# Loads, turns and stores as steps of a searched instruction order, in an attention and gated feed-forward kernel

## The chip, the cores and the metric

The kernel runs on one core of one Trainium2 chip. The metric is the device time of one execution in microseconds (us); the profile is one such execution, taken by the hardware profiler. Engines are called TensorE (PE), VectorE (DVE), ScalarE (ACT), GpSimd (POOL) and SyncE (SP). Each takes its instructions in the order in which the program lists them for it and waits on semaphores of the others.

## The reference

Input x has 4 batches of 12416 rows of 128; there are 32 inducing rows of 128. Two attention blocks and a gated feed-forward layer follow each other:

```python
def mab(q, kv):
    s = scale * (q @ kv.transpose(0, 2, 1))
    s = s - s.max(-1, keepdims=True)
    a = np.exp(s)
    a /= a.sum(-1, keepdims=True) + 1e-09
    return a @ kv
h = mab(I, x)          # per batch: 32 rows gathered from all of x
x1 = mab(x, h)         # every row of x attends to its batch's 32 rows
gate = np.maximum(x1 @ w_gate, 0.0)
val = x1 @ w_val
out = gate * val @ w_out      # 128 -> 1536 -> 128
```

So a batch's h needs all of that batch's x before any row of the batch's output can be made. The output has 49664 rows of 128 in float32.

## The kernel before

A row of x1 is a mix of only 32 rows of h, so gate times val is a quadratic form in 32 weights. The kernel uses this: for each batch it makes a table T (128 rows at a time, 8 groups of them) from h, the weights and their products, and an output tile is five matmuls of the exponentials of pairs of scores with T. This holds as long as the sign of each gate is the same for all rows of a batch; the kernel keeps a bound on that ("kept", "near"), and a general kernel stands behind a branch (L1071) that is not taken here.

**Tiles.** A batch is 97 tiles of 128 rows. Sixteen tiles make a quad q (0 to 5), the 97th tile is a small quad NQ = 6. Tiles are also counted in blocks of four (TPB), 25 blocks or slots to a batch (NSLOT).

**Stages of a batch.**
- *Load* (`load_x`, L86): a quad of x comes from HBM by a DMA that GpSimd issues, 512 KB in float32, cast on the way to the fp16 buffers x16 (nine, and two small ones).
- *Turn* (`turn_x`, L91): a quad is transposed from x16 to xT (twelve buffers) by a DMA transpose that SyncE issues. Three quads of batch 1 are turned on TensorE instead (`turn_pe`, L696).
- *First attention*: `score` (L704, L706) makes the exponentials of a quad against the inducing rows, `sums` (L716, L725) adds them up with x16, `h_end1`, `h_end2` make h.
- *Tables*: `gates`, `products` (L470), `joined` (L479), `fifth`, `table` (L516), `table5` (L536) make the next T.
- *Second attention*: `pair_scores` (L369), `pair_copy` (L634), `pair_reach` (L649), `pair_exp` (L664).
- *Outputs*: `scores` (L567, L574), called an E step, forms sums of pairs of scores for two blocks on TensorE and takes the exponential F on ScalarE. `outputs` (L589, L591), an O step, is one output tile: five matmuls into a third of an o_ps bank. After three tiles `outputs_end` divides by the sums on VectorE (L606, L607) into osb; a buffer osb holds six tiles and there are four of them. A full osb is stored by a DMA that GpSimd issues (L617), 384 KB; the last stores of all go by SyncE and ScalarE.

While the outputs of batch b are made, batch b + 1 is in its first attention and tables, and batch b + 2 is being loaded.

**The order.** The order of steps is a string, ORDER, found by a search outside the kernel. Each letter is one step: E and O as above; p takes the next step of the lane of first attention (turns on TensorE, scores, sums, h, gates, masks), u of the lane of products and tables, s of the pair scores and bounds, x of the pair exponentials. A loop at L869 walks the string and emits the instructions.

Loads, turns and stores are not in the string. They are put by hand into a dictionary `dmas`, keyed by slot, and are emitted when the first O step of that slot is reached (L875 to L877):

```python
g0 = (b - 2) * NSLOT + (0 if b > 2 else 6)
dmas[g0].append(begin)
for q in range(NCH):
    dmas[g0 + q].append(lambda q=q: load_x(b, q))
    dmas[g0 + 7 + q].append(lambda q=q: turn_x(b, turns[q]))
```

So batch 2 loads one quad per slot from slot 6 (tiles 24 to 48 of the whole run), with the small quad last, and turns one per slot after that (tiles 52 to 76), with the small quad first. Batch 3 loads at tiles 97 to 121 and turns at 125 to 149. A store is appended to the slot after the one in which its last tile falls. `begin` copies one element of the last turned quad of the batch before to a cell "landed" on GpSimd (L688), which makes GpSimd wait until that turn has landed before it issues the batch's first load.

The semaphores that an instruction waits for are put in by the framework from the buffers that it reads and writes.

Of the kernel before, what the change touches and what calls it, by code (L numbers as in the profile page):

```python
# [26 lines left out]
def quadratic_body(ctx, tc, x, inducing, moe_w_gate, moe_w_val, moe_w_out, out):  # L27
# [51 lines left out]
    def crange(q):  # L79
        return q * CT, min((q + 1) * CT, NT)  # L80
# [470 lines left out]
    NF = 20  # L551
    sel4 = sel.rearrange("p k m -> p (k m)").rearrange("p (j c) -> p j c", j=4)
    F, p2s, scs, osbs = {}, {}, {}, {}
    dmas = defaultdict(list)

    def scores(b, q, d, j):

# [38 lines left out]

    def outputs_end(b, t):
        i = t % 3
        g = b * NSLOT + t // TPB
        k = i + 1  # L600
        a = t - i
        if a % 6 == 0:
            osbs[0] = mt([P, 6, P], FP32, "osb", 4)
        osb, a6 = osbs[0], a % 6
        rz = mt([P, 3, 1], FP32, "rzo", 4)
        dve.reciprocal(out=rz[:, 0:k, :], in_=outputs.ps[:, 0:k, P : P + 1])  # L606
        dve.tensor_tensor(  # L607
            out=osb[:, a6 : a6 + k, :],
            in0=outputs.ps[:, 0:k, 0:P],
            in1=rz[:, 0:k, :].broadcast_to([P, k, P]),  # L610
            op=ALU.mult,
        )
        if a6 == 3 or t == NT - 1:
            t0 = a - a6
            last = b == B - 1 and t >= NT - 8
            queue = pool if not last else act if t == NT - 1 else nc.sync
            store = lambda: queue.dma_start(  # L617
                out=ov[b][:, t0 : t + 1, :], in_=osb[:, 0 : t + 1 - t0, :]
            )
            if last:  # L620
                store()
            else:
                dmas[g + 1].append(store)

    def pair_scores(b, q):

# [39 lines left out]
        )  # L666


    lanes = {"p": [], "u": [], "s": [], "x": []}

    def plan_scores(b):
        for q in range(0 if b else 1, NCH):
# [8 lines left out]
    def plan_phase1(b):  # L681

        s = state[b]

        def begin():

            s["x16"], s["xT"] = {}, {}
            pool.tensor_copy(out=landed, in_=state[b - 1]["xT"][2 if b == 2 else NQ - 1][0:1, 0, 0:1])  # L688

        def turn_pe(q, k):  # L690

            if k == 0:
                s["xT"][q] = new_xT(q)
            ps = bank("m", "xT_ps", [P, 8, P], FP16)
            for t in range(8):
                nc.tensor.transpose(ps[:, t, :], s["x16"][q][:, 8 * k + t, :], eye16)  # L696
            dve.tensor_copy(out=s["xT"][q][:, 8 * k : 8 * k + 8, :], in_=ps)

        def score(q):
            t0, t1 = crange(q)  # L700
            n = t1 - t0
            ps = bank("m", "s1_ps", [P, CT, M])
            for t in range(n):
                nc.tensor.matmul(ps[:, t, :], s["xT"][q][:, t, :], indT, start=True, stop=True)  # L704
            p1 = s["p1", q] = mt([P, CT, M], FP16, "p1", 3)
            act.activation(out=p1[:, 0:n, :], in_=ps[:, 0:n, :], func=AF.Exp, scale=sm_scale)  # L706

        def sums(q, first):

            t0, t1 = crange(q)  # L710
            n = t1 - t0
            k = M * min(n, 4)
            ps = bank("m", "hz_ps", [P, C + 1])
            p1 = s["p1", q]
            for t in range(0, n, 4):
                nc.tensor.matmul(  # L716
                    ps[0:k, C : C + 1],
                    p1[:, t : t + k // M, :].rearrange("p t m -> p (t m)"),
                    ones16[:, 0:1],
                    start=t == 0,  # L720
                    stop=t + 4 >= n,
                )
            for t in range(n):
                r = t % 4
                nc.tensor.matmul(  # L725
                    ps[32 * r : 32 * r + 32, 0:C],
                    p1[:, t, :],
                    s["x16"][q][:, t, :],
                    start=t < 4,
                    stop=t + 4 >= n,  # L730
                )
            if first:
                s["hz"] = mt([P, C + 1], FP32, "hz", 1)
                dve.tensor_copy(out=s["hz"], in_=ps)
            else:
                dve.tensor_tensor(out=s["hz"][0:k, :], in0=s["hz"][0:k, :], in1=ps[0:k, :], op=ALU.add)

        def h_end1():
            zs = mt([P, M], FP32, "zs", 1)
            dve.tensor_scalar(  # L740
                out=zs,
                in0=stackI,
                scalar1=s["hz"][:, C : C + 1],
                scalar2=1.0,
                op0=ALU.mult,
                op1=ALU.mult,
            )
            s["h_ps"] = bank("m", "h_ps", [P, 2, M])
            nc.tensor.matmul(s["h_ps"][:, 0, :], s["hz"][:, 0:C], stackI, start=True, stop=True)
            nc.tensor.matmul(s["h_ps"][:, 1, :], ones32, zs, start=True, stop=True)  # L750

        def h_end2():
            halves(b, s["h_ps"][:, 0, :], s["h_ps"][:, 1, :])

        turns = [NQ] + list(range(NQ))
        if b == 1:
            dmas[0] += [lambda q=q: turn_x(b, q) for q in turns[0:4]]
            lanes["p"] += [lambda h=h: turn_pe(3 + h // 2, h % 2) for h in range(6)]
            order = (3, 4, 5, NQ, 0, 1, 2)
            at = (3.5, 5.5, 7.5, 7.8, 8.5, 10.5, 12.5)  # L760
        else:
            g0 = (b - 2) * NSLOT + (0 if b > 2 else 6)
            dmas[g0].append(begin)
            for q in range(NCH):
                dmas[g0 + q].append(lambda q=q: load_x(b, q))
                dmas[g0 + 7 + q].append(lambda q=q: turn_x(b, turns[q]))
            order = (0, NQ, 1, 2, 3, 4, 5)
            at = [(2.3 if b == 2 else 3.5) * k for k in range(NCH)]
        todo = []
        for q, h in zip(order, at):  # L770
            todo.append((h, lambda q=q: score(q)))
            todo.append((h + 2, lambda q=q, h=h: sums(q, h == at[0])))
        lanes["p"] += [g for h, g in sorted(todo, key=lambda u: u[0])]
        lanes["p"] += [h_end1, h_end2]

        def gates(w, a, odd, k):
            ps = bank("m", "hw_ps", [P, BLK])
            gates_pe(b, w, k, ps)
            units = slice(k * (NFF // 2), (k + 1) * (NFF // 2))
            gates_out(act, ps.unsqueeze(1), a[:, units, :], 0)  # L780
            gates_out(dve, ps.unsqueeze(1), odd[:, units, :], 1)

        f = lambda g, *args: lambda: g(*args)
        lanes["p"] += [f(gates, *w, k) for w in ((wg, ga, gb), (wv, va, vb)) for k in range(2)]
        lanes["p"] += [lambda: (gate_sum(b, 0), signs(b)), f(gate_sum, b, 1), f(masked, b)]

        todo, late = [], []
        for j in range(4):
            for odd in range(2):
                for i in range(2):  # L790
                    todo.append(f(products, i, 0, NFF, 4 * j, 4 * j + 4, odd))
            todo.append(f(joined, j))
            late.append((len(todo) + 1, f(table, b, j)))
            if j == 1:
                todo += [f(fifth, b, 0), f(fifth, b, 1)]
                late.append((len(todo) + 1, f(table5, b)))
        for n, g in late[::-1]:
            todo.insert(n, g)
        lanes["u"] += todo
# [69 lines left out]
    for step in ORDER:  # L869
        if step == "E":  # L870
            scores(*next(units))
        elif step == "O":
            b, t = next(tiles)
            g = b * NSLOT + t // TPB
            if t % TPB == 0:  # L875
                for f in dmas.pop(g, []):
                    f()  # L877
            outputs(b, t)
            if g == B * NSLOT - 3 and t % TPB == 0:
                cond = nc.values_load(flag.left[0:1, 0:1])  # L880
        else:
            lanes[step].pop(0)()
    assert not any(lanes.values()) and not dmas and next(tiles, None) is None
    return cond


ORDER = (
    "pEpEOsEpEOOEpOEOpxOEEOuppOOEEOpsOpOEEpsOOpOEEOppOOOOEEppOOOpxsEEOOOOpEEspOOpEOOEOOEpEOpO"
    "EEpxOOOOpEEssOOOOpOEpOOEpOOOOppEEsOOEOOpEOxOOusOOEEOuOOOuEuOEOOxOOOEuEOuOOOOEsEuOuuOxEEO"
    "OuuOEsEOOEpuOuEEupupOOuEEupOuuOpOxOOEEpuOupOOOEEOpuupOEuuEuOpOuEEssOOxpOOEEspOOOEpOOEEpO"  # L890
    "OpExpEOOOOEppOOOOEEsOOOOpOEEOpOOOpOEEOpOOOpEOOEOuOOOxEuEOOOuOOuEOxOusEEOOOOusuEEOOOuOEsO"
    "OOuuuEExOOOOOuOEEuOsOuOOEEOuOuEOOxupuEEuspOOOupEEppOuOEEOuOxOuOEEpsOpOOOEEpOOOpEEOuuOOps"
    "EOEOupOsEEOuOxOOpEEpxOOOOOOEEpOOOOEOEppEOOEOOpsEExOOOOOOEEsOpOOOEEOOppOOOEEOpOOOOEpOEOxp"
    "OOOuOEEOOuOOuEOuOExOuOOOEuEOOOuEuEsOOsuOEOEOuuOEOsEuOuOsEEOOuOOOEsEuOOOEuxEEuuOOOEEuOOOO"
    "sEEOOuOOEOEuOuuOEEOOOOuEOOuEuOOxOOEEOuOsEEOxOOOOOEEOOOOOOEExOOOOOOEEsOOOEOEOOOOOEEOOOOEO"
    "OEsOEOEOOOOEEOOOxOOOEEOOOOOOEEOOOxOOOEEOOOssEOOEOOOEsEOOOOEOOEOOxOOEEsOOOOOEEsOOOOsOxEEO"
    "OOOOOOOOOOO"
)


# [202 lines left out]
```

## Time and profile before

| | |
|---|---|
| time, median of three | 279.61 us (279.19 to 279.83) |
| span of the profiled execution | 278.5 us |
| TensorE busy | 251.6 us |
| ScalarE busy | 228.1 us |
| VectorE busy | 214.5 us |
| GpSimd busy | 62.1 us |
| DMA moved | 48.38 MB, of it 38.08 MB on GpSimd's queue and 9.16 MB on SyncE's |
| E steps on ScalarE (L574) | 192 of 1025 ns |
| output tile on VectorE (L606, L607) | 132 of 175 ns and 132 of 550 ns, three tiles each |

The page gives busy time by engine, then the span in 40 slices of 7 us with the busy share of each in tenths, the clock that TensorE was granted, and the busy share of the 16 DMA engines. The list of waits says for each engine's instruction what released it: "DVE osb L607 <- DMA out_dram<-osb: 2.4, 1, 2.4" is 2.4 us in all, once, the longest 2.4. "issue" is time in which an engine waited for nothing that the profile shows. The first output tile starts at 39.3 us, the last at about 271 us.

### The profile page before, as it was taken

The page shows a single profiled execution, that of the slowest core. Times are in us where ns is not written, and L with a number is a line of the kernel's source. Part 1 is how long each engine was busy: PE and PEld are TensorE (multiplying, and loading weights), DVE is VectorE, ACT ScalarE, POOL GpSimd, SP SyncE. Part 2 cuts the span into 40 slices and gives each one's busy share as a digit, 9 for nine tenths or more (in the row PEclk, how much of TensorE's full clock was granted, in tenths as well). Part 3 has the DMA queues.
Part 4 walks back from the last instruction along what each step waited for, and adds up shares of the span by engine and source line. Part 5 has one row for each costly group of instructions (what it writes and reads, how often), then busy time and mean ns, then how long its engine had stood idle before and what let it go on. Part 6 is the DMA issues. An engine that isn't in the chain of part 4 may idle for free.

```text
span 278.5 us, 9515 instructions
## 1 busy us (share of the span) xinstructions
PE 251.6 (90%) x4029; PEld 187.7 (67%) x4029; DVE 214.5 (77%) x583; ACT 228.1 (82%) x305; POOL 62.1 (22%) x134
## 2 busy tenths in 40 slices
PE   2995799999899979998699999999999999999970
PEld 0793667777666657766387776777676777687760
DVE  4666977687899958888569989599989997767660
ACT  4235899999899969998478999999999999999930
POOL 8471000223231100431113011112121222121300
PEclk9999999999999999999779999999999999999997
DMA  7999979999979999899799992322422343424242
GB/s 184 200 208 204 214 144 143 205 201 213 244 250 203 159 209 231 162 230 261 231 218 230 149 212 112 125 114 115 172 94 79 121 174 118 169 115 172 115 170 79
DMA packets 44434, 48.38 MB, mean 174 GB/s; under 512 B 35472, under 2 KB 36272, under 8 KB 44384
## 3 DMA queue, kind: packets, MB, share of 16 engines
q0 software_dynamic: 11936, 38.08, 51.5%
q1 hardware_dynamic: 32160, 9.16, 22.4%
q8 instruction: 33, 0.54, 0.8%
q10 hardware_dynamic: 288, 0.46, 0.5%
q14 instruction: 17, 0.14, 0.1%
HBM read 27.80 MB, written 25.43 MB: 191 GB/s over the span
## 4 chain that ended last, share of the span: by engine, by line
PE 67%; DMA 8%; DVE 8%; ACT 7%; issue 5%; POOL 2%; POOLq 0%; DVEq 0%; ACTq 0%
PE o_ps L589 27%; PE e_ps L567 13%; PE o_ps L591 6%; ACT F L574 5%; DMA out_dram<-osb 4%; DMA xT<-x 4%; DVE osb L607 3%; PE s_ps L704 2%; PE T_ps L516 2%; PE xT_ps L259 2%; PE T_ps L502 2%; PE s_ps L369 2%; PE hz_ps L725 2%; PE s_ps L270 1%; PE xT_ps L696 1%
## 5 line engine op out<-in xcount | busy, mean ns | idle before, releaser
L574 ACT ACTIVATE F<-e_ps 128x1024 f16<-128x1024 f32 x192 | 185.6, 1025 | 19.9 <-PE e_ps L567 16.6
L589 PE MATMUL o_ps<-T,F 128*128 128x129 f16 x1536 | 130.5, 223 | 7.4 <-DVE osb L607 5.3
L589 PEld LDWEIGHTS <-F 128*128 128x128 f16 x1536 | 99.9, 98 | 33.9 <-issue 20.6
L591 PE MATMUL o_ps<-T,p 128*128 128x129 f16 x388 | 85.3, 220 | 0.0
L607 DVE TENSOR_TENSOR osb<-o_ps,rzo 128x384 f32<-128x384 f32 x132 | 72.5, 550 | 6.9 <-DMA out_dram<-osb 2.4
L617 POOL DMA_DIRECT2D out_dram<-osb x65 | 35.7, 549 | 187.9 <-DVE osb L607 110.4
L567 PE MATMUL e_ps<-sc,sel 32*128 32x512 f16 x384 | 59.1, 386 | 0.6
L606 DVE RECIPROCAL rzo<-o_ps 128x3 f32<-128x3 f32 x132 | 23.1, 175 | 22.7 <-PE o_ps L591 21.1
L591 PEld LDWEIGHTS <-p 128*128 128x128 f16 x388 | 38.4, 99 | 0.4
L567 PEld LDWEIGHTS <-sel 32*128 32x128 f16 x384 | 15.7, 91 | 18.0 <-issue 5.2
L634 DVE TENSOR_SCALAR sc<-s_ps 128x512 f16<-128x512 f32 (+1 forms) x28 | 17.6, 628 | 1.9 <-PE s_ps L369 1.9
L649 DVE TENSOR_REDUCE reach<-sc 128x1 f32<-128x512 f16 (+1 forms) x28 | 17.6, 627 | 1.3 <-POOL reach L648 0.3
L664 ACT ACTIVATE p<-sc 128x512 f16<-128x512 f16 (+1 forms) x28 | 16.4, 585 | 0.0
L272 ACT ACTIVATE p<-s_ps 128x256 f16<-128x256 f32 (+3 forms) x16 | 5.3, 333 | 10.9 <-PE s_ps L270 10.9
L260 DVE COPY xT<-xT_ps 128x1024 f16<-128x1024 f16 (+2 forms) x15 | 8.8, 584 | 4.5 <-PE xT_ps L259 3.2
L706 ACT ACTIVATE p<-s_ps 128x512 f16<-128x512 f32 (+1 forms) x21 | 11.3, 546 | 0.4 <-PE s_ps L704 0.2
L479 DVE TENSOR_TENSOR U<-U,U 128x1536 f16<-128x1536 f16 (+1 forms) x12 | 10.8, 903 | 0.2
L516 PE MATMUL T_ps<-wo,U 128*128 128x128 f16 x144 | 10.5, 224 | 0.2 <-DVE sc L634 0.2
L704 PE MATMUL s_ps<-indT,xT 128*128 128x32 f16 x288 | 10.0, 177 | 0.2 <-DMA xT<-x 0.2
L86 POOL DMA_DIRECT2D x<-in_x_dram x18 | 9.7, 544 | 1.8 <-DMA wg<-in_moe_w_gate_dram 1.3
L704 PEld LDWEIGHTS <-xT 128*128 128x128 f16 x288 | 8.9, 96 | 1.6 <-issue 0.9
L369 PE MATMUL s_ps<-xT,h 128*32 128x512 f16 x96 | 9.4, 387 | 0.4 <-DVE gb L361 0.4
(159 smaller groups left out, 248.2 us busy)
## 6 DMA issues: line engine op xcount, KB each, us to landing
out_dram<-osb POOLq DMA_DIRECT2D x62, 384.0 KB, 3.9
x<-in_x_dram POOLq DMA_DIRECT2D x18, 512.0 KB, 10.3
x<-in_x_dram POOLq DMA_DIRECT2D x8, 256.0 KB, 7.6
out_dram<-osb SPq DMA_DIRECT2D x2, 384.0 KB, 2.9
x<-in_x_dram POOLq DMA_DIRECT2D x5, 128.0 KB, 8.3
osb<-in_x_dram ACTq DMA_DIRECT2D x1, 384.0 KB, 4.5
osb<-in_x_dram SPq DMA_DIRECT2D x1, 384.0 KB, 4.3
wg<-in_moe_w_gate_dram POOLq DMA_DIRECT2D x1, 384.0 KB, 8.3
```

The costliest lines, as they stand in the source:

```text
L516: nc.tensor.matmul(ps, u_cols(0, t, j), wo[:, t, :], start=t == 0, stop=t == NFF - 1)
L567: nc.tensor.matmul(ps[:, r, :], sel4[rows, j, :], sc[rows, :], start=True, stop=True)
L574: act.activation(out=F[b, q, d, j], in_=ps, func=AF.Exp, scale=sm_scale2)
L589: nc.tensor.matmul(ps, f, T[b % 2][:, j, 0 : P + 1], start=j == 0, stop=False)
L591: nc.tensor.matmul(ps, p2s[b, q][rows, tok], T[b % 2][rows, 4 + r, 0 : P + 1], start=False, stop=True)
L606: dve.reciprocal(out=rz[:, 0:k, :], in_=outputs.ps[:, 0:k, P : P + 1])
L607: dve.tensor_tensor(out=osb[:, a6 : a6 + k, :], in0=outputs.ps[:, 0:k, 0:P], in1=rz[:, 0:k, :].broadcast_to([P, k, P]), op=ALU.mult,)
L617: store = lambda: queue.dma_start(out=ov[b][:, t0 : t + 1, :], in_=osb[:, 0 : t + 1 - t0, :])
L634: dve.tensor_scalar(out=scs[b, q][0:k, 0:w], in0=ps[0:k, 0:w], scalar1=64.0, scalar2=-64.0, op0=ALU.min, op1=ALU.max,)
L649: dve.tensor_reduce(out=state[b]["reach"][0:k, q : q + 1], in_=scs[b, q][0:k, 0:w], axis=AX.X, op=ALU.max, apply_absolute_value=True,)
L664: act.activation(out=p2s[b, q][0:k, 0:w], in_=scs[b, q][0:k, 0:w], func=AF.Exp, scale=sm_scale2)
L704: nc.tensor.matmul(ps[:, t, :], s["xT"][q][:, t, :], indT, start=True, stop=True)
```

## The change

Loads (letter l) and turns (t) become steps of the string; stores are emitted where their last tile ends; and the string is the result of a new search in which, by the change's own words, stores and output buffers are modelled and turned quads are allowed to land late. `dmas` and `begin` are gone.

- A load step takes the next quad in the order NQ, 0, 1, ... 5. If a turn was issued since the last load, GpSimd first waits for the latest one by the copy to "landed".
- A turn step turns the quad that was loaded last of those not yet turned (`s["loaded"].pop()`).
- Scores and sums take the quads in the order in which they were turned, not in a fixed one. The first quad summed is one that was turned first; if that were the small one, hz would be cleared.
- Batch 1's four turns by DMA are emitted before the loop.

| | before | after |
|---|---|---|
| steps | 388 O, 191 E, 82 u, 75 p, 40 s, 27 x | the same, 14 l, 14 t |
| E steps alone, in pairs | 73, 59 | 83, 54 |
| batch 2 loads before tile | 24, 28, 32, 36, 40, 44, 48 | 18, 18, 18, 18, 22, 67, 70 |
| batch 2 turns before tile | 52, 56, 60, 64, 68, 72, 76 | 44, 50, 51, 55, 57, 89, 91 |
| batch 2 scores before tile | 81, 82, 86, 90, 94, 99, 104 | 71, 76, 86, 91, 97, 114, 123 |
| batch 3 loads before tile | 97, 101, 105, 109, 113, 117, 121 | 104, 105, 111, 113, 120, 163, 166 |
| batch 3 turns before tile | 125, 129, 133, 137, 141, 145, 149 | 133, 141, 151, 151, 155, 184, 191 |
| batch 3 scores before tile | 168, 171, 171, 178, 184, 189, 194 | 166, 172, 188, 194, 207, 210, 216 |
| first, last table step of batch 1's u lane, tile | 74, 97 | 62, 93 |
| of batch 2's | 147, 191 | 161, 194 |
| of batch 3's | 248, 290 | 248, 290 |

```diff
-    dmas = defaultdict(list)
...
-            store = lambda: queue.dma_start(
-                out=ov[b][:, t0 : t + 1, :], in_=osb[:, 0 : t + 1 - t0, :]
-            )
-            if last:
-                store()
-            else:
-                dmas[g + 1].append(store)
+            queue.dma_start(out=ov[b][:, t0 : t + 1, :], in_=osb[:, 0 : t + 1 - t0, :])
...
-        def begin():
-            s["x16"], s["xT"] = {}, {}
-            pool.tensor_copy(out=landed, in_=state[b - 1]["xT"][2 if b == 2 else NQ - 1][0:1, 0, 0:1])
+        def load(q):
+            if turning:
+                pool.tensor_copy(out=landed, in_=turning[-1][0:1, 0, 0:1])
+                turning.clear()
+            load_x(b, q)
+            s["loaded"].append(q)
+
+        def turn():
+            q = s["loaded"].pop()
+            turn_x(b, q)
+            s["turned"].append(q)
+            turning.append(s["xT"][q])
...
-        def score(q):
+        def score(k):
+            q = s["turned"][k]
...
-        def sums(q, first):
+        def sums(pos):
+            q, first = s["turned"][pos], pos == 0
...
-                dve.tensor_copy(out=s["hz"], in_=ps)
+                if k < P:
+                    dve.memset(s["hz"], 0.0)
+                dve.tensor_copy(out=s["hz"][0:k, :], in_=ps[0:k, :])
...
-            dmas[0] += [lambda q=q: turn_x(b, q) for q in turns[0:4]]
+            s["turned"] += [3, 4, 5, NQ, 0, 1, 2]
+            s["xT"][3] = new_xT(3)
+            for q in (NQ, 0, 1, 2):
+                turn_x(b, q)
+            turning.append(s["xT"][2])
...
-            g0 = (b - 2) * NSLOT + (0 if b > 2 else 6)
-            dmas[g0].append(begin)
-            for q in range(NCH):
-                dmas[g0 + q].append(lambda q=q: load_x(b, q))
-                dmas[g0 + 7 + q].append(lambda q=q: turn_x(b, turns[q]))
-            order = (0, NQ, 1, 2, 3, 4, 5)
+            s["x16"], s["xT"] = {}, {}
+            lanes["l"] += [lambda q=q: load(q) for q in (NQ, *range(NQ))]
+            lanes["t"] += [turn] * NCH
...
-            if t % TPB == 0:
-                for f in dmas.pop(g, []):
-                    f()
...
 ORDER = (
-    "pEpEOsEpEOOEpOEOpxOEEOuppOOEEOpsOpOEEpsOOpOEEOppOOOOEEppOOOpxsEEOOOOpEEspOOpEOOEOOEpEOpO"
...
+    "EOpOsExpOpOEEpOOOEOOEppOEuEpOOOpEEspOOxOOpOllEElsplOOpOEEOlOOOppEEpOppOpEsEpOpOOEpOOpEpE"
+    "OOOxOsEEOOOpOpEOOpOpOtEpEOpOOEOOpOtEOEtOEuOuOOuxtOOEtusEOuOuEOOOEuuOOxEsuuEuOOOEslsOEOuu"
...
```

More of the change, by code (lines that the diff above doesn't have):

```diff
@@ L598, in outputs_end @@
         i = t % 3
-        g = b * NSLOT + t // TPB
         k = i + 1
@@ L666, in pair_exp @@
         )
-    lanes = {"p": [], "u": [], "s": [], "x": []}
+    lanes = {"p": [], "u": [], "s": [], "x": [], "l": [], "t": []}
+    turning = []
     def plan_scores(b):
@@ L683, in plan_phase1 @@
         s = state[b]
-        def begin():
-            s["x16"], s["xT"] = {}, {}
-            pool.tensor_copy(out=landed, in_=state[b - 1]["xT"][2 if b == 2 else NQ - 1][0:1, 0, 0:1])
+        def load(q):
[9 more added lines that the diff above has]
+            turning.append(s["xT"][q])
         def turn_pe(q, k):
-            if k == 0:
+            if k == 0 and q > 3:
                 s["xT"][q] = new_xT(q)
@@ L753, in h_end2 @@
             halves(b, s["h_ps"][:, 0, :], s["h_ps"][:, 1, :])
-        turns = [NQ] + list(range(NQ))
+        s["loaded"], s["turned"] = [], []
         if b == 1:
-            dmas[0] += [lambda q=q: turn_x(b, q) for q in turns[0:4]]
+            s["turned"] += [3, 4, 5, NQ, 0, 1, 2]
[3 more added lines that the diff above has]
+            turning.append(s["xT"][2])
             lanes["p"] += [lambda h=h: turn_pe(3 + h // 2, h % 2) for h in range(6)]
-            order = (3, 4, 5, NQ, 0, 1, 2)
             at = (3.5, 5.5, 7.5, 7.8, 8.5, 10.5, 12.5)
         else:
-            g0 = (b - 2) * NSLOT + (0 if b > 2 else 6)
-            dmas[g0].append(begin)
-            for q in range(NCH):
-                dmas[g0 + q].append(lambda q=q: load_x(b, q))
-                dmas[g0 + 7 + q].append(lambda q=q: turn_x(b, turns[q]))
-            order = (0, NQ, 1, 2, 3, 4, 5)
+            s["x16"], s["xT"] = {}, {}
+            lanes["l"] += [lambda q=q: load(q) for q in (NQ, *range(NQ))]
+            lanes["t"] += [turn] * NCH
             at = [(2.3 if b == 2 else 3.5) * k for k in range(NCH)]
         todo = []
-        for q, h in zip(order, at):
-            todo.append((h, lambda q=q: score(q)))
-            todo.append((h + 2, lambda q=q, h=h: sums(q, h == at[0])))
+        for k, h in enumerate(at):
+            todo.append((h, lambda k=k: score(k)))
+            todo.append((h + 2, lambda k=k: sums(k)))
         lanes["p"] += [g for h, g in sorted(todo, key=lambda u: u[0])]
@@ L882, in quadratic_body @@
             lanes[step].pop(0)()
-    assert not any(lanes.values()) and not dmas and next(tiles, None) is None
+    assert not any(lanes.values()) and next(tiles, None) is None
     return cond
 ORDER = (
-    "pEpEOsEpEOOEpOEOpxOEEOuppOOEEOpsOpOEEpsOOpOEEOppOOOOEEppOOOpxsEEOOOOpEEspOOpEOOEOOEpEOpO"
[L889 to L897, printed above, removed]
+    "EOpOsExOpOEEpOOOEOOEppOEuEpOOOpEEspOOxOOpOllEElsplOOpOEEOlOOOppEEpOppOpEsEpOpOOEEpOOpEpE"
+    "OOOxOsEEOOOpOpEOOpOpOtEpEOpOOEOOpOtEOEtOEuOuOOuxtOOEtusEOuOuEOOOEuuOOxEsuuEuOOOEslsOEOuu"
+    "OsuluEEOpOOOEEuOEpEuOpOEEuuuOOxuOOuEEssOOOxOEEpOpuOOOtEuuEupOOtpOEEOuOOOEEOppOOOEEsOOOOl"
+    "OlxEEOOpxOOOEEOlOOlOpOEEspxOOOOEEOlOOOpOEEOOOpEOEppOOEEOOpOtpEEpOOpOOOOEEOOtpOOpOEOEOOpO"
+    "EsExOOOtutOEEuOOOutOEOuussEOEOOOExuuuOOEElsOOOupluuOEsEsOOEOuxOuEEpuOpEuEuOuOxOOEEOuOOOu"
+    "uEOOEsuEuOOEEtuOOpEOuOupOEuEOOtOpEsEOOpuEEsOOOOOEEOOOxOpsEEOOOOpOOEEpOpOOOxOEEspOOpOEOpE"
+    "OEppEOOEOOppOEOppOOEpEOOOpOOEOOEpOxOOuOEEuOOOsEOuOOuusEOEOuEOOuEEuuOOOEOOOEsuEOxuOOOEEus"
+    "sOOuExuOOOxuEEsuEOuOEOOuEOOEOOOxEuEuOuOOOOEsEuOuOEEOOOOOuEEuuOOOOOEEOuOsEEOOOEOOOxOOOEEO"
+    "OOOOOEEOOxOOOOEEOOOOOOEEOOOOOxOEEOOOOOOEEsOOxOOOEEOOOOOsEEOOOOOsEEOOOOsOOEEOOOOOOEEOsOOE"
+    "OEOOOxsOOEEOOOOOEsOEOOOxOEEOOOOOOOOOOOO"
 )
```

## The prediction

> **What bounds the kernel now.** I read the page's busy times and slices first, then the loop of output tiles in three stretches, then the list of waits, then the chain and the timeline around the two places where the matmul row thins out.
>
> ```profile
> PE 251.6 (90%) x4029; PEld 187.7 (67%) x4029; DVE 214.5 (77%) x583; ACT 228.1 (82%) x305; POOL 62.1 (22%) x134
> PE   2995799999899979998699999999999999999970
> ...
> PEclk9999999999999999999779999999999999999997
> DMA  7999979999979999899799992322422343424242
> ```
>
> TensorE is the bound with ScalarE close behind. The matmul row is full but for the start, the end, and a dip in slices 19 and 20, where the granted clock dips too. The DMA engines are full until slice 24 and two thirds idle afterwards.
>
> ```profile
> 39.30:132.50 93.20, 88.09 (x1509) 64.59 (x1507) 76.55 (x204) 85.89 (x112) 21.29 (x43) 1.00 1.01 204
> 132.50:143.00 10.50, 8.04 (x70) 5.89 (x69) 5.99 (x17) 4.60 (x7) 1.34 (x3) 0.67 0.85 211
> 143.00:272.00 129.00, 125.87 (x1918) 94.40 (x1914) 105.65 (x286) 117.09 (x146) 24.04 (x51) 1.00 0.49 145
> ```
>
> The columns are window, length, then PE, weight loads, DVE, ACT and POOL busy, then granted clock, DMA share, GB/s. The loop runs from 39.3 to 272; only the middle window has a lowered clock. 0.67 over 10.5 us is 10.5 x 0.33 = 3.5 us of clock lost, or some 6.9 us at half speed.
>
> ```profile
> DVE osb L607 <- DMA out_dram<-osb: 2.4, 1, 2.4
> PE o_ps L589 <- DVE osb L607: 5.3, 9, 2.5
> PE o_ps L589 <- issue: 1.9, 2, 1.6
> PE s_ps L704 <- DMA xT<-x: 0.2, 1, 0.2
> ```
>
> ```profile
> 121.02 1.67 issue
> 122.69 0.01 POOLq L86
> 122.70 12.07 DMA out_dram<-osb
> 134.77 0.03 issue
> 134.80 0.02 DVEq L607
> 134.82 0.04 issue
> 134.87 0.57 DVE osb L607
> 135.43 0.05 issue
> 135.48 0.49 PE o_ps L589 x4
> ```
>
> This is the one large loss. A store issued at 122.70 took 12.07 us to land; VectorE wanted its buffer (osb, four of them) and waited 2.4 us; TensorE, with both o_ps banks full, stood still for 2.46 us, and the clock fell. The store is not slow by itself: L617's median from issue to landing is 8.6 us in the stretch 111 to 135 and 2.6 us in 170 to 260. Between 111.85 and 123.24 GpSimd issued six 512 KB loads of batch 3 and one small one, with four stores between; the last of these stores stood behind what was left of that.
>
> The second loss is at 97. The chain there shows a turn (DMA transpose) of 11.10 us from issue at 85.92, TensorE waiting 0.21 us for it, and then 1.64 us that the profile gives to nothing ("issue"), while the DMA share was 1.28 in 91 to 98.
>
> [...]
> - [...]
> - [...] (stores 5 to 10 us while turns run in 86 to 108, 2.6 us later).
> - [...] GpSimd's loads and stores land in the order issued all through this trace.
>
> **The change part by part.**
>
> (a) *Work.* The steps of computation are the same: 388 O, 191 E, 82 u, 75 p, 40 s, 27 x in both orders. New are 14 l and 14 t, which stand for loads and turns that were there before. The clear of hz that the diff adds is not reached, as the first quad turned of each batch is a full one. Two waits are added: the one-element copy "landed" on GpSimd now stands before the first load after any turn, four times in place of two.
>
> (b) *Loads and turns of batch 3.* Before: six loads in tiles 97 to 121, the small one last, and turns that start with the small quad, so none starts before the last load lands (135). After: four loads at tiles 105, 111, 113 and 120, the last two at 163 and 166; turns from the last loaded backwards. Between loads a store gets in. From the trace, a queued load takes 2.3 to 3.4 us of the ring and a store about 1.0 to 2.3. Four loads (11) and three stores (5) in tiles 104 to 120, which last about 14 us, leave a backlog of 2 to 4 us where before it was 12. A store also goes out at its own tile rather than at the start of the next block of four, up to three tiles earlier. Four buffers of six tiles give a store 18 tiles or more, 11 us at least. So I take the 2.46 us wait as gone, and with it the half clock. What that cost: between 135.48 and 142.50 eight tiles ran at 0.54 us in place of 0.29 (8 x 0.25 = 2.0), a table at 1.26 in place of 0.67 (0.6), other matmuls about 0.4: 3.0 us, below the 3.5 us of lost clock. Gain 5.5 us.
>
> (c) *Loads and turns of batch 2.* Before, loads in tiles 24 to 48, turns from 80.9 on (the small quad lands last), first scored at tile 81. After, four 512 KB loads at tiles 18 to 22, behind "landed", which waits for batch 1's last turn (54.5 in the trace; tile 18 comes near 50, so GpSimd stands some 4 us; behind it wait only the store of tiles 18 to 23 and later). Four loads from 55 at about 5 for the first and 2.8 each after: 68 to 70, then the store at 69 to 71. Its buffer is wanted at tile 44, at about 69.5 by the same tile's 71.0 before less some 1.5 us of E steps moved later. It is a near thing; two o_ps banks give VectorE 1 to 1.7 us, so I charge 0.3. Turns then run from about 69, four at 4.2 us each, and the earliest is scored at tile 71 (84 to 88), each with 8 us or more to spare; the last two quads load at tiles 67 and 70, turn near 97 to 105 and are scored at tiles 114 and 123 (about 121 and 127). So the wait at 97 goes. Of its 0.21 + 1.64 us I count half, 0.9, as nothing names what the larger part waited for. GpSimd's "landed" at 67, 104 and 163 meets turns that are landed or nearly so; behind it stand stores with 24 tiles of buffer.
>
> (d) *The new order of computing.* VectorE's steps priced by the rows: a tile (175 + 558)/3 = 0.24 us, a product 0.47 when back to back, a join 0.95, a pair of copy and reach 0.69 + 0.69, mask 1.5, fifth 0.75, bounds 1.0. Counted over the loop these prices give 206 us against 188 busy in the trace, so I scale by 0.91. Tiles 48 to 72 hold, after, 24 tiles (5.9), 9 products (4.2), 2 joins (1.9), 2 pairs (2.7), a mask (1.5), fifth, bounds and certain (2.4) = 18.6, scaled 16.9; TensorE's share there is 14.0 (24 x 0.29, 13 E at 0.34, tables, pairs). Tiles 144 to 168: 18.8, scaled 17.1, TensorE 14.0, ScalarE 14.6. Before, the worst such stretches are 36 to 60 and 132 to 156: 12.6 against about 12.0 each. VectorE is in order, and an output tile's copy stands behind the products, so the excess reaches TensorE, less the slack of two banks in each. (2.9 + 3.0) - 1.2 = 4.7 is the upper end, 0 the lower; I take 2.0.
>
> (e) *E steps alone or in pairs.* A pair EE takes 0.54 us before the next matmul starts, a single E 0.32, and each entry costs 0.09 more than a tile's own step. Before: 73 singles, 59 pairs. After: 83 and 54. Five pairs broken: 5 x (2 x 0.41 - 0.63) = 0.95; I take 1.0.
>
> Sum: -5.5 - 0.9 + 0.3 + 2.0 + 1.0 = -3.1: 279.6 - 3.1 = **276.5 us**.
>
> **Rivals.**
> - *Nothing given back.* Both waits go, and the new order is as even as the old: -5.5 - 1.85 = 272.3. For it: total work per engine is unchanged, and an order chosen with the stores in view need not crowd VectorE. Against: the two stretches of (d).
> - *Crowding eats the gain.* All of 4.7 and 1.0 is paid[...]: -5.5 + 0.3 + 4.7 + 1.0 = +0.5, 280.1, no change within what counts.
> - *A new late landing, slower.* The four loads at tile 18 go out back to back. In the trace one load from idle took 7.2 us (issued 55.47); at that pace the store of tiles 18 to 23 lands at 73, tile 44 waits 3 us, the clock halves again: 276.5 + 2.2 + 3.0 = 281.7. For it: DMA is full at that time (0.9 to 1.0 in 49 to 70). Against: other loads were followed at 2.4 to 3.3 us.
>
> **How the numbers follow.** Forecast 0.57; nothing given back 0.17; crowding eats it 0.10; late landing or another such stall 0.16. Faster takes the first two: 0.74. Of the third most is within 0.2% and some above: same 0.08, slower 0.18. The range runs from a little below the first rival, 272.0, to 280.8, past the second and short of the third.
>
> **What would show it.** Right: no row "osb <- DMA out_dram" in the waits, a granted clock of 1.00 from the first tile to the last, stores landing in under 10 us throughout, turns landed before their quad is scored, DMA share spread beyond 168 us, and o_ps waiting for osb a little more near tiles 50 to 70 and 150 to 168. Wrong: a gap of over 2 us on TensorE inside the loop, above all near tile 44, with a dip of the clock; or VectorE above 95% for over 10 us with TensorE waiting.

## The result, and the profile after

The changed kernel takes 288.12 us (median of four executions, 285.81 to 289.52), the kernel before 279.72 beside it. The ratio is 1.030, with an interval of 1.021 to 1.039: slower, where 276.5 had been forecast, and beyond 280.8, the upper end of the range. The ratios given here and below are of the faster executions of both kernels, as single executions of one kernel spread over several us, and so they are not the quotients of the medians.

The page of the kernel after, engines first, then the slices (7.2 us each now):

```profile
PE 259.0 (90%) x4029; PEld 193.0 (67%) x4029; DVE 214.8 (75%) x583; ACT 229.0 (80%) x305; POOL 62.2 (22%) x136
PE   2995999999797699999899499999999999999990
...
PEclk9998699999999669999999869999999999999997
```

The same 4029 matmuls keep TensorE busy 7.4 us longer, at a mean granted clock of 0.951 in place of 0.983; VectorE and ScalarE do the same work as before (214.8 and 229.0 us against 214.5 and 228.1). The dip in slices 19 and 20 has gone. In its place are two others, in slices 13 and 14 and in slice 23, and behind each the clock row falls to 6. (The smaller dip in slice 11 is taken up below, the 8 and 6 of the clock row ahead of the loop in the last section.)

The stretches of the loop in the kernel after (window, length, busy time of PE, weight loads, DVE, ACT and POOL, granted clock, DMA share, GB/s):

```profile
39.30:88.00 48.70, 46.72 (x764) 34.29 (x762) 39.80 (x103) 44.81 (x57) 8.29 (x16) 1.00 0.99 195
88.00:106.00 18.00, 13.79 (x201) 9.86 (x199) 10.24 (x28) 9.25 (x14) 3.62 (x10) 0.72 0.70 145
106.00:155.00 49.00, 47.64 (x767) 35.40 (x763) 39.07 (x106) 46.35 (x60) 10.43 (x20) 1.00 0.91 208
155.00:172.00 17.00, 13.21 (x209) 9.81 (x205) 10.88 (x31) 11.06 (x16) 3.60 (x10) 0.80 0.79 151
172.00:279.00 107.00, 105.61 (x1568) 78.76 (x1565) 88.35 (x238) 98.63 (x121) 20.91 (x42) 1.00 0.37 136
```

Two windows of 18 and 17 us carry the loss: TensorE stands still for some 4 us in each and has 0.72 and 0.80 of its clock. In both, VectorE and ScalarE are less busy too (10.2 and 9.3 of 18 us, 10.9 and 11.1 of 17), so it is no engine that is short of time. The waits of the kernel after (engine and line, releaser: us in all, times, longest) name who is missing:

```profile
POOL landed L682 <- DMA xTr<-x16r: 8.6, 2, 4.6
DVE reach L641 <- POOL reach L640: 8.2, 2, 4.4
PE T_ps L536 <- DVE lhs L530: 8.0, 2, 4.2
...
PE o_ps L588 <- DVE osb L605: 2.5, 3, 1.5
```

Three engines wait twice each, for nearly the same sum: GpSimd for a turn, VectorE for GpSimd, TensorE for VectorE. VectorE's wait for an output buffer, 2.4 us before, is 1.6 and in another place. The chain of waits of the kernel after shows the links in order (start, us, what):

```profile
89.27 3.31 DMA xTr<-x16r
...
92.72 0.16 POOL landed L682
...
93.24 0.54 POOL x L86
...
93.80 0.26 POOL ok L439
...
94.50 0.05 POOL reach L640
...
94.57 0.69 DVE reach L641
95.26 0.17 DVE lhs L529
...
95.46 0.27 DVE lhs L530
...
95.77 1.47 PE T_ps L536 x48
```

`reach` at L640 is `pool.memset(state[b]["reach"], 0.0)`, 0.1 us of work: before the first of a batch's seven pair steps writes its column of `reach`, GpSimd clears the tile. It stands in GpSimd's stream where that pair step stands in the string. In the new string load steps come shortly before: `...OOOEslsOEOuuOsulu...` has a load at tile 67, then the "s" of `certain` (ok, near, kept on GpSimd), then the "s" that clears at tile 70; `...OOEElsOOOupluuOEs...` has loads at 163 and 166 and the clear at 167. The first load waits for the turn in flight (L682). So the clear, which needs nothing from it, is held until that turn has landed; VectorE's reduction of the first pair (L641) waits for the clear; behind it in VectorE's stream are the operands of a table (L529, L530); and TensorE stands at the table's matmuls (L536), which start at 95.77, with the output tiles behind them from 97.17. GpSimd stood for 4.0 us at this wait, until the turn had landed at 92.6, and TensorE lost 4.21 us at 91.56. The second time GpSimd stood for 4.6 us, and TensorE lost 3.79 us at 161.40.

In the loop the granted clock was 0.50 for 10.24 us from 95.25 and for 6.83 us from 163.51; the first 0.5 and 1.7 us of that still fell into the gaps. From the first output tile to the last the loop takes 241.4 us, against 232.2 in the profiled execution of before.

### The profile page after: what moved, and what is told of

It is laid out like the page before. It is cut to its first block, busy times and chain, and to the rows that moved or that the text cites. A ratio compares the mean times of both kernels' runs of the same rounds, so it can differ in the third digit from the quotient of the medians.

```text
span 287.1 us, 9528 instructions
## 1 busy us (share of the span) xinstructions
PE 259.0 (90%) x4029; PEld 193.0 (67%) x4029; DVE 214.8 (75%) x583; ACT 229.0 (80%) x305; POOL 62.2 (22%) x136
## 4 chain that ended last, share of the span: by engine, by line
PE 56%; DMA 23%; DVE 7%; ACT 4%; POOL 3%; issue 2%; SPq 2%; POOLq 0%; DVEq 0%; ACTq 0%
PE o_ps L588 27%; PE e_ps L566 12%; DMA x16r<-in_x_dram 6%; PE o_ps L590 6%; DMA out_dram<-osb 5%; DMA xT<-x 3%; DMA wv<-in_moe_w_val_dram 3%; ACT F L573 3%; PE T_ps L516 3%; DMA xTr<-x16r 3%; DMA x<-in_x_dram 3%; DVE osb L605 3%; SPq L91 2%; PE s_ps L369 2%; PE s_ps L708 1%
## 5 line engine op out<-in xcount | busy, mean ns | idle before, releaser
L588 PE MATMUL o_ps<-T,F 128*128 128x129 f16 x1536 | 132.1, 224 | 3.0 <-DVE osb L605 2.5
L588 PEld LDWEIGHTS <-F 128*128 128x128 f16 x1536 | 100.7, 99 | 30.1 <-issue 20.6
L566 PE MATMUL e_ps<-sc,sel 32*128 32x512 f16 x384 | 60.8, 390 | 0.5 <-ACT F L573 0.3
L641 DVE TENSOR_REDUCE reach<-sc 128x1 f32<-128x512 f16 (+1 forms) x28 | 17.6, 627 | 9.2 <-POOL reach L640 8.2
L479 DVE TENSOR_TENSOR U<-U,U 128x1536 f16<-128x1536 f16 (+1 forms) x12 | 10.9, 905 | 0.4
L536 PE MATMUL T_ps<-wo,lhs 128*32 128x128 f16 x144 | 3.8, 281 | 8.0 <-DVE lhs L530 8.0
L502 PE MATMUL T_ps<-won,U 128*128 128x128 f16 x96 | 8.0, 257 | 2.5 <-DVE U L470 2.5
L502 PEld LDWEIGHTS <-U 128*128 128x128 f16 x96 | 7.3, 118 | 4.2 <-DVE U L470 4.1
## 6 DMA issues: line engine op xcount, KB each, us to landing
x<-in_x_dram POOLq DMA_DIRECT2D x18, 512.0 KB, 10.2
```

The lines of the kernel that those rows point to most:

```text
L502: nc.tensor.matmul(s["T_ps"][j // 2][:, j % 2, :], u_cols(i, t, j), won[:, t, :], start=False, stop=(i, t, j % 2) == (1, NFF - 1, 1),)
L566: nc.tensor.matmul(ps[:, r, :], sel4[rows, j, :], sc[rows, :], start=True, stop=True)
L588: nc.tensor.matmul(ps, f, T[b % 2][:, j, 0 : P + 1], start=j == 0, stop=False)
L641: dve.tensor_reduce(out=state[b]["reach"][0:k, q : q + 1], in_=scs[b, q][0:k, 0:w], axis=AX.X, op=ALU.max, apply_absolute_value=True,)
```

## The experiments

Theory 1: the clear of `reach`, queued on GpSimd behind a wait for a turn, starves VectorE and so TensorE, and the half clock adds to the loss. Theory 2: the new order crowds VectorE, as step (d) of the prediction had it, and the gaps only show where. Theory 3, in the expectations: the late turns themselves hold up the scores that need them. One more thing to test is what the prediction counted as the gain, the late store of before.

Each kernel ran beside the kernel before, on the same chip. The first four shared 19 executions of before (median 280.2 us), the other four another 19 (280.39). Ratios are to these. The ratios carry the verdicts: where the interval lies wholly on one side of 1, the kernel is faster or slower, and by how much is known only within it. The profiles show where the gaps are.

**The clear on VectorE**, its consumer, and nothing else:

```diff
-            pool.memset(state[b]["reach"], 0.0)
+            dve.memset(state[b]["reach"], 0.0)
```

> The changed kernel, with the clear of reach on VectorE instead of GpSimd; nothing else moves. Theory 1, the clear of reach stood on GpSimd behind the wait for a landed turn: the two gaps of TensorE, 4.21 us near 91 and 3.79 us near 161, go, the half clock after them goes with them, and the time falls by 10 to 13 us from 288.1, to 275 to 278, below the 279.7 of the kernel before. Theory 2, VectorE is crowded in tiles 48 to 72 and 144 to 168: reach starts sooner, but VectorE is as late as it was; the gaps shrink by no more than a third, 284 to 287. Theory 3, the late turns themselves hold the work up: the gaps move to the scores that need the turned quads, 285 to 288.

Measured: 275.92 us, ratio 0.988 (0.979 to 0.998). GpSimd still waits 4.2 us for a turn at 157, and in the loop no compute engine waits for GpSimd any more: the rows of L641 and of T_ps at L536 are gone from the waits. (At the first place it came to the wait late in this execution and did not stand, so this profile tests the second place alone.) One statement of 0.1 us takes the kernel from 3% slower to 1.2% faster. What is left is in the waits of this kernel:

```profile
PE o_ps L588 <- DVE osb L605: 3.8, 3, 2.8
...
DVE osb L605 <- DMA out_dram<-osb: 2.9, 1, 2.9
```

The store of tiles 18 to 23 is late: TensorE stands for 2.82 us at 72.54, with half clock for 13.65 us from 76.60 (this execution took 280.26 us, the second longest of seven). This is the rival of a late landing. In the kernel after itself it is smaller, as the chain there shows:

```profile
58.06 0.18 POOL landed L682
...
60.91 13.51 DMA out_dram<-osb
...
74.51 0.57 DVE osb L605
```

GpSimd was released at 58.06, when batch 1's last turn had landed, issued the small load and four large ones until 60.9, and the store behind them took 13.51 us; TensorE lost 1.52 us and no clock.

**No wait before the loads.** The clear stays on GpSimd:

```diff
             if turning:
-                pool.tensor_copy(out=landed, in_=turning[-1][0:1, 0, 0:1])
                 turning.clear()
```

> The changed kernel without the one-element copy landed on GpSimd, in all four places; nothing reads its result, and each transfer keeps the waits for its own buffers. Left out is only that GpSimd holds its next load until the last turn has landed. Theory 1: the clear of reach is no longer held, the two gaps go, 275 to 279; loads may now run beside turns and land a few us later. Theory 2: gaps stay, 284 to 287. Theory 3: turns take longer beside the loads, and gaps move to the scores; 284 to 290.

Measured: 273.63 us, a little under the range expected, ratio 0.982 (0.972 to 0.991). With the wait gone the clear is on time where it was, on GpSimd: in the profiled execution no gap of TensorE inside the loop reaches 0.7 us, and the clock is 1.00 in all of it. The loads of batch 2 go out at 54.2 in place of 58.3, so the store that follows them is not late either: it takes 13.7 us to land, but at 71.5 in place of 74.4, and VectorE does not wait for it. The turns are in time for their scores without the wait, against theory 3.

This kernel has the instructions and the order of the changed one, less four copies of one element, and so it prices the loss. Its loop takes 225.6 us with 3.2 of TensorE idle, that of the changed kernel 241.4 with 12.7. Of the 15.8 us between them 9.5 are idle time, just the three gaps (4.21 + 3.79 + 1.52), and the other 6.3 are the same matmuls taking longer. In the changed kernel four of an output tile (L588) take 0.61 us at 99.65, at half clock, and 0.40 at 90.22. An estimate from its 17.1 us of half clock: 14.9 of them lie outside the gaps and can cost 7.4 at most.

**The clear on VectorE in the kernel before**, as a control, since the clear might be worth moving by itself:

> The kernel before with the clear of reach on VectorE; a control. There the clear waited 0.3 us at most. Theory 1: no change, within 0.5 us of 279.7. If the clear on GpSimd were costly in itself[...], this kernel would gain 1 us or more too.

Measured: 281.62 us, 1.4 above before by the medians, ratio 1.002 (0.995 to 1.009): no difference that counts, and no gain. (One of its 14 executions took 535.97 us; nothing here explains it.) In the kernel before VectorE waited for a clear once, 0.3 us, by the trace: with the old order no wait for a turn holds one up for longer. It is the order of the change that makes it dear.

**Order alone.** The changed kernel with three load steps moved behind the pair step that clears, and nothing else: the load of tile 67 goes behind the "s" of tile 70, those of tiles 163 and 166 behind the "s" of tile 167.

```diff
-    ...OOOEslsOEOuu" "OsuluEEO...
+    ...OOOEssOEOuuO" "sluluEEO...
-    ...OOEElsOOOupluuOEsEsOOEO...
+    ...OOEEsOOOupuuOEsEsllOOEO...
```

> The changed kernel with three letters of its order moved and nothing else: batch 2's fifth load step goes from tile 67 to just behind the pair step of tile 70 that clears reach, and batch 3's last two go from tiles 163 and 166 to just behind that of tile 167. The clear stays on GpSimd and the wait for the landed turn stays. Theory 1: the place of the clear behind that wait is the whole cause; 274 to 278, as with the clear on VectorE. If moving work from GpSimd to VectorE was what helped, the time stays at 285 to 288.

Measured: 278.36 us, just above the range expected, ratio 0.997 (0.989 to 1.004): level with before. GpSimd's timeline in this kernel (start, us, engine, line, operation, tile) has the clear ahead of the wait:

```profile
93.94 0.09 POOL L640 MEMSET reach<- 128x7 f32 x1
94.00 0.17 POOL L682 CAST landed<-xTr 1x1 f32<-1x1 f16 x1
```

Both gaps at L536 are gone. The second place is the test: there GpSimd stood 1.5 us at the wait with the clear already done. At the first the loop was late enough for the turn to have landed. The gap of the late store stays (2.06 us at 73.83, half clock for 10.24 us from 76.9, in an execution of 279.52 us). So the place of three letters in a string of 831 made the 3%; in this execution the store at tile 44 holds back the rest of the gain.

**Five output buffers.** In the kernel before this takes away the wait whose end the prediction priced at 5.5 us; in the changed kernel it takes away most of the wait for the late store and leaves the clear where it is; with the clear on VectorE it is meant to take away both.

```diff
-            osbs[0] = mt([P, 6, P], FP32, "osb", 4)
+            osbs[0] = mt([P, 6, P], FP32, "osb", 5)
```

(and the same number where the two buffers of the start are taken from this pool)

> The kernel before with five output buffers in place of four. It sizes the term of the prediction for the late store near 133. If the 2.46 us gap and the half clock after it cost 5.5 us: 274 to 275. If ScalarE or VectorE had set the pace there anyway: 277 to 279. No change (279.7) would say that something else releases TensorE there.

Measured: 275.58 us, between the first two ranges expected, ratio 0.987 (0.977 to 0.997): 3.6 us by the ratio, 4.6 by the medians. The interval runs from 0.8 to 6.5 us, so 5.5 is not ruled out.

> The changed kernel with five output buffers, the clear left on GpSimd. Theory 1: the two gaps of 4 us stay, only the 1.5 us gap near 73 goes; 284 to 287. If output buffers were the main cause, 274 to 278.

Measured: 288.02 us, just above the range of theory 1, ratio 1.035 (1.024 to 1.047), as slow as the changed kernel. The gap at 73.6 has shrunk to 0.4 us, and the waits of this kernel keep the two of the clear, with the longer one longer:

```profile
DVE reach L641 <- POOL reach L640: 9.6, 2, 6.2
...
PE T_ps L536 <- DVE lhs L530: 9.3, 2, 6.0
```

The turn that GpSimd waits for lands at 92.0 here and at 92.6 in the changed kernel. What TensorE gains at the store it loses again at the clear, where it now stands for 6.03 us from 89.19.

> The changed kernel with the clear of reach on VectorE and five output buffers. The run with the clear alone still had a gap of 2.8 us near 73, where the store of tiles 18 to 23 landed 14 us after issue behind four loads. If that gap is the buffer's: it goes, and 272.5 to 274. If the turns are at the root: no change, 274.5 to 276.

Measured: 274.43 us, between the two ranges expected, ratio 0.984 (0.975 to 0.994), close to the kernel without the waits for turns. This is the clearest separation of the wait from what stands behind it. GpSimd stands for turns about twice as long as in the changed kernel (start, us, instruction, and the idle time before it with what ended it):

```profile
96.63 0.17 POOL L682 CAST landed<-xTr 1x1 f32<-1x1 f16 x1 [9.14 <-DMA xTr<-x16r]
...
155.64 0.53 POOL L682 CAST landed<-xTr 1x1 f32<-1x1 f16 x1 [7.14 <-DMA xTr<-x16r]
```

TensorE has no gap of more than 0.92 us in the loop all the same. That one is a score which waits 0.9 us for a turn, and is all that theory 3 finds in any of these profiles of the new order.

**All three**: clear on VectorE, no wait before the loads, five buffers.

> The changed kernel with all of it: clear on VectorE, no wait for a landed turn, five output buffers. Theory 1: no gap of over 1 us is left in the loop, 271.5 to 273.5, faster than the kernel before by 2% or more.

Measured: 273.6 us, just above the range expected, ratio 0.982 (0.972 to 0.992), so 2% is not shown. It does no better than leaving out the wait alone. This fits the traces, in which one wait is behind both losses of the new order: the wait for turns on GpSimd delayed the clear and, by 4 us, the loads that delayed the store. Both versions beat the two given kernels.

It also answers theory 2. The two stretches that step (d) feared, from the first matmul of tile 48 to that of tile 72 and from 144 to 168, are these in this kernel:

```profile
74.56:89.65 15.09, 15.05 (x195) 10.44 (x194) 14.56 (x43) 13.95 (x19) 3.42 (x8) 1.00 0.99 231
133.64:147.87 14.23, 14.14 (x188) 9.78 (x186) 13.71 (x38) 13.87 (x17) 2.94 (x6) 1.00 1.16 219
```

VectorE is busy 14.56 of 15.09 us in the first, and TensorE is at work 15.05 of them. TensorE's waits for VectorE's output copy are down from the 5.3 us of before:

```profile
PE o_ps L588 <- DVE osb L605: 1.0, 2, 0.6
```

Theory 2 falls: VectorE is nearly full there, but has no more to do than TensorE, and no gap comes of it.

## Why the prediction was wrong

- **The step that failed is the last sentence of (c)**: "GpSimd's 'landed' at 67, 104 and 163 meets turns that are landed or nearly so; behind it stand stores with 24 tiles of buffer." The first half was too hopeful: at 67 and 163 GpSimd waited 4.0 and 4.6 us (at 104 not at all). The prediction had batch 2's turns run from 69 at 4.2 us each; the loads went out at 58.3 in place of 55, and the turns ran from 73.5 at 4.7. The second half was wrong, and it made the loss. Behind the wait stood also the bounds' small operations and the clear of `reach`, and not a store but VectorE was the one who waited, with no buffer between. TensorE lost 4.21 and 3.79 us, and 17.1 us of half clock came with it. Taking away the wait (273.63), moving the clear off GpSimd (275.92), or moving the loads behind the clear (278.36) each undoes the slowdown; a fifth buffer for the stores (288.02) doesn't. The prediction had counted GpSimd's queue as loads and stores, when the string and `pair_reach` together place the clear behind the load.
- **No rival had it**, though one sign of being wrong came true: gaps of over 2 us on TensorE, at 91.56 and 161.40 and not near tile 44. The slow rival, a late landing of the store of tiles 18 to 23, is real but smaller: predicted landing 73 and 3 us of waiting with half clock; measured 74.4 and 1.52 us without half clock in the kernel after, 2.82 and 2.06 us with it in two of its variants. With the two gaps of the clear gone (order alone) it leaves the kernel level with before, and not 2 us slower.
- **(b) was right in kind; its size is open.** The store of batch 3 is no longer late, and no clock is lost near 133. Its worth was 3.6 to 4.6 us by the two measures, with an interval that holds the 5.5. Executions of before differ in it (the control's profile, at 276.05, has a gap of 1.37 us there and no half clock).
- **(c), batch 2's turns**: right that the wait at 97 goes: no score waits for a turn in the kernel after. GpSimd's wait at tile 18 came out as said (4.3 us), but later: tile 18 comes at 53.5 in the trace of before, not near 50, and the turn landed at 58.0 in the kernel after, not at 54.5.
- **(d) is a term with nothing in it**, in place of +2.0, and what failed is the sum of its prices. For the two stretches it had 16.9 and 17.1 us of VectorE against 14.0 of TensorE. The version with all three changes has 14.56 and 13.71 against 15.05 and 14.14: there is no surplus that could reach TensorE. In its whole loop TensorE idles 3.5 us against 9.9 in the kernel before, and waits 1.0 us for output copies against 5.3.
- **(e)**, +1.0 for single E steps, was not measured by itself. An estimate from the medians and ratios puts a bound on it and (d): the gains of (b) and of the wait at 97, 3.6 to 4.6 us measured and 0.9 to 1.85 by the prediction, make 4.5 to 6.4, and the new order without its waits gains 5.2 us by its ratio (0.0185 x 280.2). So (d) and (e) together cost about 1 us or nothing by these figures, but each gain has an interval of some 5 us, and this is not shown. Nor do the runs tell the forecast of 276.5 from the rival "nothing given back", 272.3: without the waits the new order gives 0.972 to 0.991 of 279.6, which is 271.8 to 277.1.

## What to carry to other kernels

Before you put a wait into an engine's stream, list all that stands behind it there until the wait can end, and who waits for each: the smallest instruction counts as much as the largest, and a 0.1 us clear of a tile held up three engines here. Give set-up work such as clears to the engine that uses the tile, or put it well ahead of the wait; an engine that issues transfers and sits idle four fifths of the time is a poor place for it if it also waits for transfers. And read a search's model by what it leaves out: by the change's own words this one had stores, buffers and late turns in it; the time went to a thing without a letter of its own, the clear within "s". Whether the model had that too is not on record.

## What the runs showed of the hardware that was not expected

- In these profiles a lowered clock (0.50 in the given kernels) outlasted the gap ahead of it, and in one of them it cost more than the gap. In the loop of the kernel after, the gaps of 4.21 and 3.79 us were followed by 10.24 and 6.83 us of half clock; elsewhere a gap of 2.82 us by 13.65 (the clear on VectorE), one of 2.46 by 6.83 (the kernel before), one of 2.06 by 10.24 (order alone), and ones of 1.64 (the kernel before), 1.52 (the kernel after) and 1.37 us (the control) by none. A gap of 1.53 us was followed by 3.41 us where a half-clock stretch had ended 1.8 us before it (the kernel before with five buffers, at 171.28). Nor does the length of a gap alone tell: ahead of the loop, TensorE stands for 2.53 us in both given kernels, and in the kernel after the clock is 0.50 for 6.83 us from 26.98, inside that gap, while in the kernel before it stays at 1.00. The stretches in the loop, 3.41, 6.83, 10.24 and 13.65 us, are 1, 2, 3 and 4 times the shortest. The loop with the gap of 2.82 us takes 233.8 us, 8.2 more than that of the version without the wait; 2.8 of these are idle time, which leaves 5.4 for the clock.
- The gap of 1.64 us at 97.6 in the kernel before, put down to "issue", stays unexplained, and there are larger ones: the kernel before with five buffers has one of 3.56 us at 162.0 in its profiled execution (285.38 us, its longest), and half clock follows it: the mean granted clock of that execution is 0.967, against 0.983 in the profiled one of before. No run here was aimed at it.
- A store of 384 KB that takes 2.6 us in the quiet stretch of before (the median from 170 to 260) took 13.51 us behind four loads of 512 KB and one of 32 KB, issued in the 2.6 us before it. GpSimd's 103 transfers land in the order in which they were issued in the traces of both given kernels. The sizes are as the profile counts them, of the fp16 data that land; in float32 a quad is twice as large, 1 MB.
